# Sparse attention with a two-layer Mish network: a third set of PSUM banks for the last two blocks, and the last second product in half products

## The chip, the cores and the metric

One NeuronCore of one Trainium2 chip runs the whole program. The metric is the device time of one execution in microseconds (us): 319.56 us before the change, the median of 3 runs (319.44 to 320.93).

## The reference

Cut to what matters (8 batches, 8 heads, 576 positions, head size 64; 512 model columns, 2048 hidden ones):

```python
scores = np.matmul(q, k.transpose(0, 1, 3, 2)) / np.sqrt(64)
scores = np.where(masks, scores, -1e9)      # heads 0-3: the last 32 positions; heads 4-7: every 32nd
attn = softmax(scores)                      # over the last axis
x = (attn @ v).transpose(0, 2, 1, 3).reshape(4608, 512)
h = x @ w_in                                # 512 -> 2048: the first product
g = h * np.tanh(softplus(h))                # Mish
out = g @ w_out                             # 2048 -> 512: the second product
```

## The kernel before

The 4608 rows are cut into 9 blocks of 512 (t = 0 to 8). Attention works on one batch at a time and writes its result, transposed and in bf16, to `xT`; by the time that block 7 begins all 8 batches are done, so blocks 7 and 8 have only the network left.

**Seven products for eight.** Both matrix products use a scheme with seven products of half matrices where the plain way has eight (with sums of halves ahead and behind). The first product of a block is done in four groups g = 0 to 3 of 512 hidden columns. Each of its seven products is 4 matmuls of 128x128 by 128x256, so a group has 28 and a block 112. The second product has seven products n = 1 to 7 of 16 matmuls each (two halves u = 0, 1 of 8), again 112 in a block. Sums for the left and right sides are made on VectorE (DVE): `x_sum` from `xT` into `xs`, `g_sum` from `gT` into `gs`.

**Banks.** PSUM has 8 banks here: two sets of three, `SETS[0]` = (be0, al0, ee0) and `SETS[1]` = (be1, al1, ee1), and two banks of the attention, at0 and at1 (`A0`, `A1`). A group of the first product (`Mlp1.step`, L391) needs one bank each for be, al and ee: product 5 goes to ee and is copied to `s5`; product 1 goes to al and is copied to be by ScalarE (ACT, L401); product 6 is added to al and that copied to `s2`; 3 is added to ee, and DVE adds `s2` to it into `hh` (L119); 2 is added to be; 7 is added to al, and DVE adds `s5` to it into `hh`; 4 is added to al. Then ACT takes Mish of be ("U", L418), al ("W", L420) and `hh` ("H", L414) into `gT`. In the plan these steps are called a (products 5, 1), b (6, 3, 2), c (7), d (4). A word such as `b2` is step b of group 2. `SETS`, `s2`, `s5` and `hh` are chosen by z = (t + g + 1) % 2, so groups alternate between two sets.

The second product (`Mlp2.half`, L456) of the block ahead runs in the same stretch of the program, its 14 half products called `m` in the plan. It uses the three banks of one set: 1 starts al and ACT copies it to be (L477), 5 starts ee and is copied to `o5` (L479), 2 is added to be, 6 is added to al and copied to `o2` (L481), 3 is added to ee, 7 and 4 to al. DVE adds `o2` and `o5` into the output tile `osb`, ACT copies be and al (L490, L491), and SP stores 256 rows of 512 columns at a time (L501, 512 KB).

**Order.** It is written by hand. `run(plan, t)` (L662) issues the words of a plan one after the other, and every engine works through its own instructions in that order, waiting only where one needs another's result or space. `PLAIN` (L741) is the plan of t = 7 and t = 8:

```python
PLAIN = ("m m x0 m x1 m x2 g1 g2 m m m m g3 m m m m a0 m m b0 a1 x3 c0 U0 b1 d0 U1 W0 c1 a2 d1 W1 H0 "
         "a3 b2 c2 H1 b3 c3 d2 W2 H3 d3 n U2 U3 W3 H2")
```

After t = 8 the second product of block 8 stands alone (L749 to L756), in the order 1, 5, 6, 2, 7, 3, 4. Its last copy (L491) and the store behind it end the kernel.

Of the kernel before, what the change touches and what calls it, by code (L numbers as in the profile page):

```python
# [10 lines left out]
F32 = mybir.dt.float32  # L11
# [34 lines left out]
def kernel(ctx, tc, q, k, v, moe_w_in, moe_w_out, out):  # L46
    nc = tc.nc
    B, H, S, D = q.shape
# [4 lines left out]
    NBLK = NT // 512  # L53
    RT = RING * S
    PE, Po, Dv, Sc = nc.tensor, nc.gpsimd, nc.vector, nc.scalar
# [16 lines left out]
    s2, s5 = [[sb([128, 512], f"{n}{i}", F32) for i in range(2)] for n in ("s2", "s5")]  # L72
    o2, o5 = sb([128, 512], "o2", F32), sb([128, 512], "o5", F32)
    hh = [sb([128, 2, 512], f"hh{i}", F32) for i in range(2)]
# [33 lines left out]
    SETS = [[bank(f"{n}{i}") for n in ("be", "al", "ee")] for i in range(2)]  # L108
    A0, A1 = bank("at0"), bank("at1")
    PAIRS = ((A0, A1), SETS[0][1:3], SETS[1][1:3])  # L110

    def cast(eng, out_, in_):
        if eng is Sc:
# [4 lines left out]
    def add(eng, out_, a, b, op=ALU.add):  # L118
        eng.tensor_tensor(out=out_, in0=a, in1=b, op=op)  # L119
# [250 lines left out]
    class Mlp1:  # L370
# [19 lines left out]

        def step(self, s, g):  # L391
            z = (self.t + g + 1) % 2
            h = hh[z]
            be, al, E = [x[:] for x in SETS[z]]
            o = gT[:, 4 * g:4 * g + 4, :]
            two = lambda x: x.rearrange("p (u n) -> p u n", u=2)
            if s == "a":
                self.prod(5, g, E, True)
                cast(self.eng, s5[z][:], E)
                self.prod(1, g, al, True)  # L400
                Sc.copy(be, al)  # L401
            elif s == "b":
                self.prod(6, g, al, False)
                cast(self.eng, s2[z][:], al)
                self.prod(3, g, E, False)
                add(Dv, h[:, 0, :], E, s2[z][:])
                self.prod(2, g, be, False)
            elif s == "c":
                self.prod(7, g, al, False)
                add(Dv, h[:, 1, :], al, s5[z][:])  # L410
            elif s == "d":
                self.prod(4, g, al, False)
            elif s == "H":
                Sc.activation(  # L414
                    o[:, :, 256:512], h[:].rearrange("p i (u n) -> p (i u) n", u=2), AF.Mish
                )
            elif s == "U":
                Sc.activation(o[:, 0:2, 0:256], two(be), AF.Mish)  # L418
            elif s == "W":
                Sc.activation(o[:, 2:4, 0:256], two(al), AF.Mish)  # L420
# [15 lines left out]
    class Mlp2:  # L436
# [19 lines left out]
        def half(self, n, u):  # L456
            z = (self.t + 1) % 2
            be, al, E = [x[:] for x in SETS[z]]
            W = lambda kk, j: w_out[:, 8 * kk:8 * kk + 8, 256 * j:256 * j + 256]
            G = self.G  # L460
            L, R, bank, start = {
                1: (G(0, 0), W(0, 0), al, True), 2: (G(0, 1), W(1, 0), be, False),
                3: (G(1, 1), wos[:, 2], E, False), 4: (gs[:, 1], W(1, 1), al, False),
                5: (gs[:, 0], W(0, 1), E, True), 6: (gs[:, 1], wos[:, 0], al, False),
                7: (gs[:, 2], wos[:, 1], al, False),
            }[n]
            for c in range(8):
                mm(
                    bank[:, 256 * u:256 * u + 256], L[:, c, 128 * u:128 * u + 128], R[:, c, :],
                    start=(start and u == 0 and c == 0), stop=(c == 7),  # L470
                )
            if u == 0:
                return
            r = 512 * self.t
            halves = lambda x: x.rearrange("p (u d) -> p u d", u=2)
            if n == 1:
                Sc.copy(be, al)  # L477
            elif n == 5:
                Sc.copy(o5[:], E)  # L479
            elif n == 6:  # L480
                Sc.copy(o2[:], al)  # L481
            elif n == 3:
                osb = self.out_tile(1)
                add(Dv, osb[:, :, 0:256], halves(E), halves(o2[:]))
            elif n == 7:
                osb = self.out_tile(1)
                add(Dv, osb[:, :, 256:512], halves(al), halves(o5[:]))
            elif n == 4:
                osb = self.out_tile(0)
                Sc.copy(osb[:, :, 0:256], halves(be))  # L490
                Sc.copy(osb[:, :, 256:512], halves(al))  # L491
                self.store(0)
# [8 lines left out]
            nc.sync.dma_start(out[r:r + 256, :].rearrange("(u p) d -> p u d", u=2), self.osb[i][:])  # L501

        def steps(self, order=(1, 5, 2, 6, 3, 7, 4)):
            last = max(order, key=lambda n: order.index(n) if n in (3, 7) else -1)

            def go(n, u):
                self.half(n, u)
                if (n, u) == (last, 1):
                    self.store(1)
            return [lambda n=n, u=u: go(n, u) for n in order for u in range(2)]  # L510

    with tc.manual_schedule():
# [7 lines left out]
        def unread(n, to, w=512):  # L520
            for _ in range(n):
                mm(to[:, 0:w], wis[:, 0, 0, 0, 0:128], wis[:, 0:2, 0, 0, 0:w // 2], True)
# [139 lines left out]
        def run(plan, t):  # L662
            b = t + 1
            m1, m2, nxt = Mlp1(t), Mlp2(t - 1), Mlp2(t)
            at = Attn(b) if b < B else None
            ms = m2.steps() if t > 1 else []
            bank = [0]

            def v_steps():
                def pv(kind, r):  # L670
                    at.pv(kind, *r, (A0, A1)[bank[0] % 2])
                    bank[0] += 1

                def xt(kind, hf):
                    at.xt(kind, hf, (A0, A1)[bank[0] % 2], Dv)
                    bank[0] += 1
                P = lambda kd, r: (lambda: pv(kd, r))
                X = lambda kd, hf: (lambda: xt(kd, hf))
                return (
                    [P("s", r) for r in PV_S] + [X("s", 0), X("s", 1)]  # L680
                    + [P("l", r) for r in PV_L[:2]] + [X("l", 0)]
                    + [P("l", r) for r in PV_L[2:]] + [X("l", 1)]
                )
            vs_ = v_steps() if at else []
            JOBS = [("s", 0), ("s", 1), ("s", 2), ("l", 0), ("l", 1), ("l", 2)]
            for w in plan.split():
                c, n = w[0], int(w[1:]) if len(w) > 1 else 0
                if c in "abcdHUW":
                    m1.step(c, n)
                elif c == "p":  # L690
                    plain(t, n, six[n % 6], act=False)
                elif c == "y":
                    Sc.activation(gT[:, n, :], six[n % 6][:], AF.Mish)  # L693
                elif c == "k":
                    w_in_sums(2 * (n % 2), 2 * (n % 2) + 2, Dv, n // 2)
                elif c == "m":
                    ms.pop(0)()
                elif c == "x":
                    x_sum(t, n, Dv)
                elif c == "g":  # L700
                    m2.g_sum(n, Dv)
                elif c == "n":
                    nxt.g_sum(0, Dv, 0, 8)
                elif not at:
                    continue
                elif c == "e":
                    Sc.preload_act_table(AF.Exp)
                elif c == "f":
                    Sc.preload_act_table(AF.Mish)
                elif c == "q":  # L710
                    at.qk(*JOBS[n], PAIRS[n % 2 * (1 + (t + 1) % 2) if t > 1 else 0])
                    at.mask(*JOBS[n], Po)
                elif c == "v":
                    if vs_:
                        vs_.pop(0)()
                elif c == "s":
                    spread_v(Dv)
                    share_v(b, Dv)
                elif b + 1 >= B:
                    continue  # L720
                elif c == "D":
                    transpose_by_dma()
                elif c == "V":
                    load_vs(b + 1)
                    load_vl(b + 1)
                elif c == "R" and b + 2 < B:
                    load_qk(b + 2)
            assert not ms
            for w in vs_:
                w()  # L730
# [8 lines left out]
            "p11 y6 v p12 y7 v p13 y8 v p14 y9 v p15 y10 y11 y12 y13 y14 y15 n k1 k3 k5 k7"  # L739
        )  # L740
        PLAIN = (  # L741
            "m m x0 m x1 m x2 g1 g2 m m m m g3 m m m m a0 m m "
            "b0 a1 x3 c0 U0 b1 d0 U1 W0 c1 a2 d1 W1 H0 a3 b2 c2 H1 b3 c3 d2 W2 H3 d3 n U2 "
            "U3 W3 H2"
        )

        for t in range(1, NBLK):
            run(SECOND if t == 1 else MAIN if t + 1 < B else PLAIN, t)
        last = Mlp2(NBLK - 1)  # L749
        st = last.steps((1, 5, 6, 2, 7, 3, 4))  # L750
        last.g_sum(1, Dv)
        last.g_sum(2, Dv)
        for n, s in enumerate(st):
            s()
            if n == 5:
                last.g_sum(3, Dv)  # L756


# [28 lines left out]
```

## Time and profile before

| | |
|---|---|
| Median of 3 runs | 319.56 us |
| The profiled execution | 319.21 us |
| its span, first to last instruction | 317.4 us |
| mean granted TensorE clock | 0.983 |
| TensorE (PE) busy, whole span | 288.6 us (91%) |
| DVE, ACT busy, whole span | 205.7 us (65%), 201.2 us (63%) |
| Block 7's stretch (iteration t = 7) | about 245.8 to 272.5 us |
| Block 8's stretch (iteration t = 8) | about 272.5 to 299.2 us |
| Second product of block 8, alone | 299.2 to 312.6 us |
| Last copy, last store, end | 312.6 to 317.4 us |

How to read the profile: "L125 PE" are the matmuls (one helper line for all), "PEld" the weight loads, and `al<-xs,wis` names what is written and what is read, with the buffer numbers left out. `[0.28 <-ACT be L401]` after a row means that the engine sat idle for 0.28 us before it until ACT's instruction of line 401 on `be` was done. The profile models the end of a matmul: four matmuls of 256 columns show 0.60 us, while the next four start 0.44 us after them when nothing is waited for. So the true pause of PE between two rows is taken from their starts: the distance, less 0.109 us for each matmul of the first row.

### The profile page before, as it was taken

How to read it: one execution, taken by the hardware profiler on the slowest of the kernel's cores; microseconds unless marked ns; L12 is line 12 of the kernel's file. 1: busy time of each engine (PE TensorE's matmuls, PEld its weight loads, DVE VectorE, ACT ScalarE, POOL GpSimd, SP SyncE). 2: the span in 40 equal slices, each digit the busy share in tenths (PEclk: the TensorE clock that was granted, in tenths of full speed). 3: DMA queues.
4: the chain of work that ended last, by engine and by line, in shares of the span. 5: the costliest groups of instructions: out<-in, count | busy, mean ns of one | idle time of the engine just before them, and what ended most of it. 6: DMA issues, size and time to landing. Idle time of an engine off the chain costs nothing.

```text
span 317.4 us, 7701 instructions
## 1 busy us (share of the span) xinstructions
PE 288.6 (91%) x3218; PEld 228.4 (72%) x3224; DVE 205.7 (65%) x378; ACT 201.2 (63%) x357; POOL 116.9 (37%) x94
## 2 busy tenths in 40 slices
PE   8879679986994999999999999999999999999983
PEld 3554356833473798888888888988898887787773
DVE  2370396833888578768867794779578657747641
ACT  2587364357461768987887888788868526625630
POOL 8422355349504680298049607800930000000000
PEclk9999998999899899999999999999999999999999
DMA  7999999998990899589939993990030030002003
GB/s 105 182 206 206 204 183 138 95 243 130 150 115 0 114 231 169 32 142 214 169 41 176 205 137 64 213 107 0 2 134 2 0 119 15 3 34 101 0 2 133
DMA packets 97555, 35.85 MB, mean 113 GB/s; under 512 B 80800, under 2 KB 92896, under 8 KB 97520
## 3 DMA queue, kind: packets, MB, share of 16 engines
q0 software_dynamic: 60192, 17.67, 61.7%
q1 hardware_dynamic: 37184, 17.57, 27.7%
q8 instruction: 25, 0.41, 0.5%
q10 hardware_dynamic: 144, 0.12, 0.1%
q14 instruction: 10, 0.08, 0.1%
HBM read 35.51 MB, written 9.44 MB: 142 GB/s over the span
## 4 chain that ended last, share of the span: by engine, by line
PE 58%; DVE 16%; ACT 10%; DMA 10%; issue 4%; POOL 1%; DVEq 0%; ACTq 0%; POOLq 0%
PE al L125 29%; PE ee L125 14%; PE be L125 8%; DMA hh<-in_k_dram 7%; DVE hh L119 4%; DMA ql<-in_q_dram 3%; DVE gs L119 3%; ACT s L114 2%; ACT gT L414 2%; PE at L294 2%; PE at L125 2%; ACT gT L420 2%; DVE x_l L303 2%; DVE wis L119 1%; ACT be L401 1%
## 5 line engine op out<-in xcount | busy, mean ns | idle before, releaser
L125 PEld LDWEIGHTS <-w_in 128*128 128x128 bf16 x576 | 53.9, 98 | 23.6 <-issue 9.2
L271 POOL TENSOR_TENSOR Ps<-Ps,consts_sb 72x864 bf16<-72x864 bf16 (+1 forms) x20 | 36.8, 1859 | 87.1 <-ACT Ps L265 87.1
L125 PEld LDWEIGHTS <-gs 128*128 128x128 bf16 x576 | 55.8, 99 | 13.3 <-DVE gs L119 5.8
L125 PEld LDWEIGHTS <-gT 128*128 128x128 bf16 x432 | 41.0, 98 | 6.7 <-issue 0.4
L125 PE MATMUL al<-wos,gs 128*128 128x256 bf16 x288 | 36.4, 278 | 5.4 <-DVE gs L119 5.3
L125 PEld LDWEIGHTS <-wis 128*128 128x128 bf16 x348 | 33.1, 99 | 7.9 <-issue 3.3
L119 DVE TENSOR_TENSOR gs<-gT,gs 128x2048 bf16<-128x2048 bf16 x18 | 25.2, 1398 | 20.0 <-PE al L125 15.1
L271 POOL TENSOR_TENSOR Pl<-Pl,consts_sb 128x960 bf16<-128x960 bf16 (+1 forms) x20 | 33.5, 1701 | 0.8 <-ACT Pl L265 0.7
L125 PE MATMUL al<-xs,wis 128*128 128x256 bf16 x224 | 32.4, 272 | 0.8 <-ACT be L401 0.6
L125 PE MATMUL be<-xT,w_in 128*128 128x256 bf16 (+1 forms) x157 | 30.1, 311 | 2.8 <-ACT gT L693 1.3
L414 ACT ACTIVATE gT<-hh 128x1024 bf16<-128x1024 f32 x28 | 29.8, 1065 | 0.0
L125 PE MATMUL al<-xT,w_in 128*128 128x256 bf16 (+1 forms) x150 | 27.1, 299 | 1.9 <-ACT gT L420 1.7
L298 DVE RECIPROCAL rden<-at 72x7 f32<-72x7 f32 (+2 forms) x60 | 11.2, 187 | 21.6 <-PE at L294 18.1
L401 ACT COPY be<-al 128x512 f32<-128x512 f32 x28 | 16.4, 587 | 12.5 <-PE al L125 12.5
L420 ACT ACTIVATE gT<-al 128x512 bf16<-128x512 f32 x28 | 16.8, 599 | 11.0 <-PE al L125 11.0
L119 DVE TENSOR_TENSOR gs<-gT 128x2048 bf16<-128x2048 bf16 x18 | 21.9, 1217 | 0.0
L119 DVE TENSOR_TENSOR hh<-al,s 128x512 f32<-128x512 f32 x28 | 19.2, 684 | 2.9 <-PE al L125 2.5
L119 DVE TENSOR_TENSOR hh<-ee,s 128x512 f32<-128x512 f32 x28 | 19.2, 684 | 2.8 <-ACT s L114 1.9
L303 DVE TENSOR_TENSOR x_s<-at,rden 72x448 bf16<-72x448 f32 (+1 forms) x35 | 20.1, 574 | 1.2
L125 PE MATMUL ee<-wos,gT 128*128 128x256 bf16 x144 | 18.7, 277 | 0.0
L418 ACT ACTIVATE gT<-be 128x512 bf16<-128x512 f32 x28 | 15.9, 596 | 3.9 <-PE be L125 3.9
L125 PE MATMUL al<-xs,w_in 128*128 128x256 bf16 x112 | 16.8, 272 | 1.6 <-DVE hh L119 1.6
(137 smaller groups left out, 537.7 us busy)
## 6 DMA issues: line engine op xcount, KB each, us to landing
out_dram<-osb SPq DMA_DIRECT2D x18, 512.0 KB, 3.4
vraw<-in_v_dram POOLq DMA_DIRECT2D x8, 288.0 KB, 7.4
vl<-in_v_dram POOLq DMA_DIRECT2D x8, 288.0 KB, 9.6
w_in<-in_moe_w_in_dram POOLq DMA_DIRECT2D x4, 512.0 KB, 15.4
w_out<-in_moe_w_out_dram POOLq DMA_DIRECT2D x2, 1024.0 KB, 21.7
ql<-in_q_dram POOLq DMA_DIRECT2D x7, 288.0 KB, 12.9
kl<-in_k_dram POOLq DMA_DIRECT2D x5, 384.0 KB, 12.6
ks<-in_k_dram POOLq DMA_DIRECT2D x6, 288.0 KB, 10.0
```

Source lines behind the costliest of these rows:

```text
L114: Sc.copy(out_, in_)
L119: eng.tensor_tensor(out=out_, in0=a, in1=b, op=op)
L125: PE.matmul(o, lhsT=lhsT, rhs=rhs, start=start, stop=stop, skip_group_check=True)
L271: meng.tensor_tensor(out=pm, in0=pm, in1=mk[0:n, :].unsqueeze(1).unsqueeze(1).to_broadcast([n, 2, nu, w]), op=ALU.mult,)
L294: PE.matmul(po[:, n - n0, :], lhsT=pt[0:r, c0:c0 + 128], rhs=rhs, start=True, stop=True)
L298: Dv.reciprocal(rden[0:m, 0:nu], po[0:m, :, D])
L303: Dv.tensor_tensor(out=x[0:m, n0:n1, :], in0=po[0:m, :, 0:D], in1=rden[0:m, 0:nu].unsqueeze(2).to_broadcast([m, nu, D]), op=ALU.mult,)
L401: Sc.copy(be, al)
L414: Sc.activation(o[:, :, 256:512], h[:].rearrange("p i (u n) -> p (i u) n", u=2), AF.Mish)
L418: Sc.activation(o[:, 0:2, 0:256], two(be), AF.Mish)
L420: Sc.activation(o[:, 2:4, 0:256], two(al), AF.Mish)
```

## The change

It touches what is issued from t = 7 on.

- A third set of buffers is made as views of `ks` and `qs`, which hold rows of the attention: `hh[2]`, `s2[2]`, `s5[2]`. For t = 7 and 8 (`self.eng is Dv`), group 1 takes at1 as be, at0 as al, the ee bank of the set of group 0, and these buffers. Groups 0, 1, 2, 3 then have the buffers (t+1)%2, 2, t%2, (t+1)%2.
- At t = 7 one matmul of 512 columns is added that writes at1 (`unread(1, A1)`).
- `PLAIN` gets another order: the steps of the first product's groups 0 and 1 stand between the `m` of the second product, `x3` and `g1` stand earlier, and the last steps are ordered anew.
- The last second product (block 8) runs in half products: 1, 1, 5, 5, 2 (first half), 6, 6, 2 (second half), 7, 7, 3 (first half), 4, 4, 3 (second half). The second halves of 5 and 3 go to at0. Its output is stored in five pieces as they come: two of 128 rows by 256 columns from SP (product 3), three of 256 rows by 256 columns issued by ACT (products 2, 7, 4). Products 5 and 3 are copied or added 256 columns at a time.

```diff
+    wide = lambda x: flat(x[:].bitcast(F32))
+    hh.append(wide(ks).rearrange("p (i n) -> p i n", i=2))
+    s2.append(wide(qs)[:, 0:512])
+    s5.append(wide(qs)[:, 512:1024])
...
             z = (self.t + g + 1) % 2
+            be, al, E = [x[:] for x in SETS[z]]
+            if self.eng is Dv:
+                z = ((self.t + 1) % 2, 2, self.t % 2, (self.t + 1) % 2)[g]
+                be, al, E = [x[:] for x in ((A1, A0, SETS[(self.t + 1) % 2][2]) if g == 1 else SETS[z])]
             h = hh[z]
-            be, al, E = [x[:] for x in SETS[z]]
...
+            end = self.t == NBLK - 1
+            fresh = u == 0
+            if end and u and bank is E:
+                bank, fresh = A0[:], True
...
+            if end and n in (3, 5):
+                w = slice(256 * u, 256 * u + 256)
+                if n == 5:
+                    Sc.copy(o5[:, w], bank[:, w])
+                else:
+                    osb, r = self.out_tile(1), 512 * self.t + 256 + 128 * u
+                    add(Dv, osb[:, u, 0:256], bank[:, w], o2[:, w])
+                    nc.sync.dma_start(out[r:r + 128, 0:256], osb[:, u, 0:256])
+                return
             if u == 0:
                 return
-            r = 512 * self.t
+            if end and n in (2, 4, 7):
+                osb, k, r = self.out_tile(n == 7), slice(256 * (n > 2), 256 * (n > 2) + 256), 512 * self.t
+                src = (be if n == 2 else al).rearrange("p (u d) -> p u d", u=2)
+                if n == 7:
+                    r += 256
+                    add(Dv, osb[:, :, k], src, o5[:].rearrange("p (u d) -> p u d", u=2))
+                else:
+                    Sc.copy(osb[:, :, k], src)
+                Sc.dma_start(out[r:r + 256, k].rearrange("(u p) d -> p u d", u=2), osb[:, :, k])
+                return
...
+            if b == B:
+                unread(1, A1)
...
         PLAIN = (
-            "m m x0 m x1 m x2 g1 g2 m m m m g3 m m m m a0 m m "
-            "b0 a1 x3 c0 U0 b1 d0 U1 W0 c1 a2 d1 W1 H0 a3 b2 c2 H1 b3 c3 d2 W2 H3 d3 n U2 "
-            "U3 W3 H2"
+            "m m x0 g1 x1 m x2 x3 a0 m m m g2 m m b0 m g3 m m m c0 U0 a1 H0 m m b1 d0 W0 a2 c1 a3 b2 b3 d1 c3 "
+            "U2 H1 W1 U1 c2 d3 W3 U3 n d2 H2 W2 H3"
         )
...
-        st = last.steps((1, 5, 6, 2, 7, 3, 4))
+        st = last.steps("10 11 50 51 20 60 61 21 70 71 30 40 41 31")
...
-            if n == 5:
+            if n == 6:
                 last.g_sum(3, Dv)
```

More of the change, by code (lines that the diff above doesn't have):

```diff
@@ L469, in half @@
                     bank[:, 256 * u:256 * u + 256], L[:, c, 128 * u:128 * u + 128], R[:, c, :],
-                    start=(start and u == 0 and c == 0), stop=(c == 7),
+                    start=(start and fresh and c == 0), stop=(c == 7),
                 )
+            if end and n in (3, 5):
[7 more added lines that the diff above has]
+                return
             if u == 0:
                 return
-            r = 512 * self.t
+            if end and n in (2, 4, 7):
[8 more added lines that the diff above has]
+                return
             halves = lambda x: x.rearrange("p (u d) -> p u d", u=2)
@@ L503, in steps @@
         def steps(self, order=(1, 5, 2, 6, 3, 7, 4)):
+            if isinstance(order, str):
+                return [lambda n=int(w[0]), u=int(w[1]): self.half(n, u) for w in order.split()]
             last = max(order, key=lambda n: order.index(n) if n in (3, 7) else -1)
```

## The prediction

> **What bounds the kernel now.** I read the page's busy shares first, then the busy times by stretch for the part that the change touches, then the instructions in order of time in that part, then the end: the last store in the DMA view. Up to 245.8 us every engine's instructions are the same before and after, in the same order, so only 245.8 to the end (71.6 us of the span) can move.
>
> The stretches of blocks 7, 8 and the closing second product (length; then busy time of PE, PEld, DVE, ACT, POOL; PE's granted clock; DMA share; GB/s):
>
> ```profile
> 245.80:272.50 26.70, 25.56 (x227) 21.89 (x225) 18.34 (x27) 12.92 (x22) 0.00 (x0) 1.00 0.11 40
> 272.50:299.20 26.70, 25.52 (x226) 21.85 (x224) 17.92 (x27) 12.92 (x22) 0.00 (x0) 1.00 0.11 41
> 299.20:312.80 13.60, 12.58 (x114) 10.80 (x112) 5.63 (x6) 5.59 (x10) 0.00 (x0) 1.00 0.03 9
> ```
>
> PE is the bound: DVE works 18 of 26.7 us, ACT 13, DMA a tenth. The clock is full, so a matmul of 256 columns takes its 0.109 us (16 of them 1.75 us from start to start). A block has 224, which is 24.4 us; it takes 26.7. The 2.3 us between are pauses of PE, in which it waits for a copy, an add or a Mish. Those of block 8, in order of time (start, length, engine, line):
>
> ```profile
> 288.05 0.60 PE L125 MATMUL al<-xs,wis 128*128 128x256 bf16 x4
> 288.30 0.57 ACT L401 COPY be<-al 128x512 f32<-128x512 f32 x1 [1.65 <-PE al L125]
> ...
> 288.92 0.60 PE L125 MATMUL al<-xs,wis 128*128 128x256 bf16 x4 [0.28 <-ACT be L401]
> ...
> 293.45 0.60 PE L125 MATMUL al<-xT,w_in 128*128 128x256 bf16 x4 [0.35 <-ACT gT L420]
> ...
> 297.36 0.60 PE L125 MATMUL al<-xs,wis 128*128 128x256 bf16 x4
> ...
> 297.79 0.60 PE L125 MATMUL al<-xs,w_in 128*128 128x256 bf16 x4
> 298.05 0.68 DVE L119 TENSOR_TENSOR hh<-al,s 128x512 f32<-128x512 f32 x1
> ...
> 298.78 0.60 PE L125 MATMUL al<-xs,w_in 128*128 128x256 bf16 x4 [0.39 <-DVE hh L119]
> ...
> 303.69 1.92 PE L125 MATMUL al<-wos,gs 128*128 128x256 bf16 x16 [0.82 <-DVE gs L119]
> ...
> 312.64 0.59 ACT L491 COPY osb<-al 128x512 f32<-128x512 f32 x1 [4.61 <-PE al L125]
> ```
>
> The reader is to see the shape of a pause: a group of 4 is done, a reader starts 0.24 us after its last slot, works 0.6 to 0.7 us, PE may write again 0.05 us later, and between stands one other group (0.44 us). From start to start the pauses of block 8 are 0.21 (ahead of product 2 of the second product, at 276.19), 0.07, 0.44 (288.92), 0.09, 0.52 (293.45), 0.14, 0.28 (297.36), 0.55 (298.78): 2.30. Block 7 has the same eight, 2.26. The closing product has one, 0.99 (303.69), where product 6 waits for `gs`. Together **5.55 us**.
>
> **The change, part by part.** I laid the new order of each engine beside its waits and went through it with the durations of these rows: matmul 0.109; PE to reader 0.24; ACT on 512 columns 0.59, the next one 0.48 after its start; Mish of `hh` 1.06; DVE on 512 columns 0.69, the next one 0.60 after its start, 0.80 if it needs the first; `gs` 1.22; back to PE 0.05. The same way through the old order gives 5.4 of the 5.55 us of pauses, each in its place, so the method is good to some 0.15 us here.
>
> *What goes.* Groups 0 and 1 of a block no longer share banks with the second product of the block ahead (that has set t%2, they have the other set and at0, at1), so their steps stand between its halves, and each pause's cover grows from one group to at least a half product. Product 2 (0.21): eight matmuls of step a stand ahead, 0.87 more. Step b after the copy of line 401 (0.44): a0 and b0, and a1 and b1, now have at least 16 matmuls (1.75 us) between them where 0.88 is needed. Step a3 after "W" (0.52): d0's last matmul and a3's product 1 have 16 between. The small ones (0.09, 0.14, 0.28, 0.07) go the same way. Closing product (0.99): 8 matmuls of product 2 stand ahead of product 6, and the Mish order at the block's end is another; `gs` is ready 0.25 us ahead of its use.
>
> *What is late next.* At each block's end three pauses stay. The last writes are c3, c2, d3, d2: d3 waits for DVE's add on c3's bank, 0.24 + 0.69 + 0.05 = 0.98 after c3, with 0.44 of c2 as cover: 0.54, the pause of 298.78 again. d2 waits for the next add, which ends 0.60 after the first; d3 covers 0.44: 0.16. The second product's product 1 takes d3's bank, which ACT reads first: 0.24 + 0.59 + 0.05 = 0.88, with 0.16 + 0.44 as cover: 0.28. Together 0.98 a block, 1.96 for two. In the closing product 4 waits for the add of 7 (0.98, covered by 8 matmuls, 0.87): 0.10. The nearest waits without a pause have 0.16 (product 2 on the copy to be), 0.24 and 0.25 us to spare. Beyond `unread` the count of matmuls is the same; that one has 512 columns, 0.22 (four such rows start 0.86 apart early in the span). PE's term: 5.55 - 1.96 - 0.10 - 0.22 = **3.3 us**; from the old walk instead of the trace 3.15. I take 3.2. With hand-offs shorter or longer by 0.05 us it is 2.8 to 3.6: longer hand-offs hurt the old order more.
>
> *At nothing.* The sums moved ahead (`x3`, `g1`) lie on DVE, 8 us idle a block. The two copies of 256 columns for product 5 and the ACT stores lie where ACT idles: 4.61 us ahead of its last copy. A store holds its issuer 0.37 us (SP's rows). The ACT store of product 7 waits for DVE's add with the copy for product 4 queued behind it; that copy needs matmuls which end 1.7 us after the add. Without this cover it would cost up to 0.4.
>
> *The end.* T is the last matmul's slot end (310.69 + 16 x 0.109 = 312.43). Before, ACT copies from T + 0.2, the store is issued at T + 0.8 (313.25) and lands 3.1 later; the span ends 1.1 after that. The DMA views of the stretch 313 to 313.5 (packets, MB, share of 16 engines; then KB and us to landing), and SP's rows of the last two stores:
>
> ```profile
> q1 hardware_dynamic: 94, 0.19, 100.4%
> ...
> out_dram<-osb SPq DMA_DIRECT2D x1, 512.0 KB, 3.1
> ```
>
> ```profile
> 311.61 2.01 SPq L501 DMA_DIRECT2D out_dram<-osb  x2
> ```
>
> One store keeps all 16 engines busy: 94 packets of 2 KB in 0.5 us, 85 ns each on 16 engines. The store's 256 packets are 16 an engine, 1.36 us of its 3.1; the first moves 1.5 after the issue. After, the last piece is an add of 256 columns: 384 columns take 0.55 (L303), 512 take 0.69, so 0.41; it is issued at T + 0.7, 128 packets of 1 KB. The piece of product 4 (256 packets) was issued from ACT at T + 0.1. No row has 1-KB packets on this queue: half of 85 (43 ns) is the floor, the whole 85 the ceiling. The page's part 3 has the queue's rest: of 37184 packets, 17.57 MB and 27.7% of 16 engines' span, 4608 are these of 2 KB; the others have 250 bytes and 31 ns on the mean. On the line between, 1 KB takes 54, which I take. Both pieces are 24 packets an engine: from T + 1.6, 1.3 us, and 0.25 for the rest: landed at T + 3.1 where it was T + 3.9. **0.8 us** gained, 0 at 85 ns, 1.1 at 43.
>
> The Trainium skill, "DMA: Bandwidth & Descriptors", section "Issuing engines are not separate DMA queues", says that transfers issued from different engines interleave on the same 16 DMA engines and that only issue time is saved. It speaks against the two issuers: by it the pieces add up, as above; were ACT's queue apart, the last piece (8 packets an engine) would land at T + 2.9 and the gain be 1.0. The row with 100.4% for one store points the same way, but no run here shows two queues at once.
>
> **Sum.** 3.2 + 0.8 = 4.0 us. The profiled execution took 319.21 (span 317.4 and 1.8 around it), which gives **315.2**. The median of the runs is 0.35 above that execution, inside their spread of 1.5.
>
> **Rivals.** (1) *The end gives nothing*: 1-KB packets cost as 2-KB ones, or the pieces queue. For it: no row of their size. Against it: the line between the queue's short and long packets. 315.2 + 0.8 = 316.0. (2) *The pauses come back in other places*: groups 0 and 1 share one ee bank, group 1's al and be are the only spare pair, and DVE takes all copies to `s2`, `s5` in strict order behind the 1.22-us sums. If half of the 3.5 us that went come back, 317.0; if all, no change, about 319. For it: four waits have 0.25 us or less to spare. Against it: each is crossed with rows of the same instruction. (3) *Slower: DVE falls behind.* Place: DVE's queue in the first half of the block, where the sums `gs` and `xs` now stand ahead of the copies that free ee and al. PE has some 28 hand-overs in two blocks with 0.4 us to spare on the mean; if each comes 0.6 late, PE loses 28 x 0.2 = 5.6 us, as much as the 4.0 gained plus 1.6, the 0.5% that a measurement of this kernel can tell from no change. Under 0.55 late it isn't slower. That needs DVE's 0.69 to become nearly twice as long; the trace has it at 0.68 to 0.69 whatever else runs. If it decides: about 321. (4) *The change doesn't do what it says*, since an engine's order keeps the old wait: the orders as built show the moves, so this is a part of rival 2.
>
> **How the numbers follow.** Forecast 0.70, rival 1 0.11, half of the pauses back 0.09, no change 0.05, slower 0.05. Faster by over 0.5% is forecast, rival 1 and half: 0.90; the same 0.05; slower 0.05. Range: PE at 3.6 and the end at 1.1 give 319.21 - 4.7 = 314.5, and 0.3 less for the spread of runs, 314.2; upwards it takes rivals 1 and half of 2: 317.0.
>
> **What would show it.** In the trace after: no pause of PE over 0.1 us within a block until its last four groups, then 0.54, 0.16, 0.28; the last matmul 3.2 us earlier (312.4 to 309.2); product 6 of the closing product without a wait on `gs`; the last store landing 3.1 after the last matmul's slot instead of 3.9. Wrong it is if PE shows pauses in the first half of block 7 or 8 (rival 2 or 3), or if packets of 1 KB take 85 ns (rival 1).

## The result, and the profile after

315.25 us, the median of 4 runs (314.98 to 316.73), beside 320.15 before (4 runs, 319.44 to 320.93). The ratio is 0.9856, 95% interval 0.9814 to 0.9898. In a second set (`after_again`, below) it was 314.77 (5 runs) beside 320.43 (17 runs), 0.9838, interval 0.981 to 0.9867. The kernel is about 5 us, some 1.5%, faster.

The profiled execution took 314.98 us, its span 313.2. Busy times of the changed kernel by stretch, cut at the first matmul of block 6's second product (246.69, in before 245.80) and at the last matmul's slot end T (309.78, in before 312.44) (length; then busy time and instructions of PE, PEld, DVE, ACT, POOL; PE's granted clock; DMA share; GB/s):

```profile
0.00:16.00 16.00, 12.57 (x146) 6.18 (x147) 4.34 (x20) 6.22 (x11) 10.45 (x17) 0.89 1.15 144
16.00:40.00 24.00, 21.49 (x193) 11.69 (x194) 9.11 (x24) 15.36 (x31) 7.22 (x9) 0.86 1.26 204
...
246.69:309.78 63.09, 62.22 (x561) 54.66 (x559) 41.20 (x58) 32.13 (x53) 0.00 (x0) 1.00 0.12 45
309.78:313.20 3.42, 0.17 (x2) 0.00 (x0) 0.43 (x1) 0.00 (x0) 0.00 (x0) 0.98 0.34 115
```

The same stretches of before, which the prediction did not show:

```profile
0.00:16.00 16.00, 13.59 (x138) 6.72 (x140) 4.24 (x20) 6.23 (x11) 10.74 (x17) 1.00 1.12 144
16.00:40.00 24.00, 19.18 (x200) 10.67 (x202) 9.28 (x24) 15.58 (x32) 7.61 (x9) 1.00 1.25 205
...
245.80:312.44 66.64, 63.50 (x562) 54.53 (x559) 41.89 (x58) 31.26 (x51) 0.00 (x0) 1.00 0.09 33
312.44:317.40 4.96, 0.16 (x2) 0.00 (x0) 0.00 (x0) 0.59 (x1) 0.00 (x0) 0.94 0.56 213
```

Three things are to be read off. From the first of those matmuls to T it is 63.1 us where it was 66.6: 3.5 less, against which stands the 0.2 of the added matmul, issued ahead of the stretch. From T to the end it is 3.4 where it was 5.0: 1.6 less. Together 4.9. And the part that the change does not touch is no constant: blocks 7 and 8 began 0.9 us later in this execution than in the one of before, and the change accounts for the added matmul's 0.2 alone. (So T is 309.8, and not the 309.2 that the prediction names.) Over eleven profiled executions that start lay between 245.8 and 248.6 us, and the one of before was the earliest. PE's clock early in the span differs too (0.86 against 1.00 from 16 to 40 us), but that it is the whole cause is not shown; the last section comes back to it. So I compare kernels by these two stretches, and by medians. The stretches hold still: 63.09 and 63.08 up to T in two executions of the changed kernel, and 3.38 to 3.41 behind T in five with its closing product.

The changed kernel's instructions in order of time, at the end of block 7 and at the kernel's end (here and below, a view's last row counts only the instructions inside its window):

```profile
269.40 1.04 PE L129 MATMUL al<-xs,wis 128*128 128x256 bf16 x8
...
270.78 1.20 PE L129 MATMUL al<-xs,w_in 128*128 128x256 bf16 x8 [0.34 <-DVE hh L123]
...
271.38 0.31 PEld L129 LDWEIGHTS <-w_in 128*128 128x128 bf16 x3 [0.17 <-issue]
...
272.07 1.14 PE L129 MATMUL al<-w_out,gT 128*128 128x256 bf16 x9
```

```profile
301.80 1.91 PE L129 MATMUL al<-wos,gs 128*128 128x256 bf16 x16
...
307.17 1.91 PE L129 MATMUL al<-w_out,gs 128*128 128x256 bf16 x16
...
309.98 0.43 DVE L123 TENSOR_TENSOR osb<-at,o 128x256 f32<-128x256 f32 x1 [2.32 <-PE at L129]
```

From start to start (the eight matmuls of 269.40 take 0.87, those of 270.78 too), PE pauses 0.51 before 270.78, 0.16 in the midst of that row, where its weight loads stop at 271.38, and 0.25 before 272.07. These are step d of group 3, step d of group 2 and the next second product, as in the prediction. Block 8 has the same three. Product 6 of the closing product (301.80) waits for nothing; product 4 (307.17) waits 0.13. All the pauses from 246.7 on are 1.97 us, where there were 5.54.

### The profile page after: what moved, and what is told of

It is laid out like the page before. It is cut to its first block, busy times and chain, and to the rows that moved or that the text cites. A ratio compares the mean times of both kernels' runs of the same rounds, so it can differ in the third digit from the quotient of the medians.

```text
span 313.2 us, 7708 instructions
## 1 busy us (share of the span) xinstructions
PE 289.6 (92%) x3225; PEld 229.1 (73%) x3225; DVE 205.9 (66%) x379; ACT 201.6 (64%) x358; POOL 116.6 (37%) x94
## 4 chain that ended last, share of the span: by engine, by line
PE 62%; DVE 15%; DMA 10%; ACT 8%; issue 3%; POOL 1%; DVEq 0%; POOLq 0%; ACTq 0%
PE al L129 30%; PE ee L129 15%; PE be L129 9%; DMA hh<-in_k_dram 7%; PE at L129 4%; DVE hh L123 4%; DMA ql<-in_q_dram 3%; ACT s L118 2%; DVE gs L123 2%; PE at L298 2%; DVE x_l L307 2%; ACT gT L427 1%; DVE wis L123 1%; ACT gT L421 1%; DVE x_s L307 1%
## 5 line engine op out<-in xcount | busy, mean ns | idle before, releaser
L129 PE MATMUL al<-xs,wis 128*128 128x256 bf16 x208 | 30.1, 272 | 0.0
L421 ACT ACTIVATE gT<-hh 128x1024 bf16<-128x1024 f32 x26 | 27.7, 1064 | 0.0
L427 ACT ACTIVATE gT<-al 128x512 bf16<-128x512 f32 x26 | 15.5, 598 | 9.2 <-PE al L129 9.2
L123 DVE TENSOR_TENSOR hh<-al,s 128x512 f32<-128x512 f32 x26 | 17.6, 684 | 2.7 <-PE al L129 2.1
L123 DVE TENSOR_TENSOR hh<-ee,s 128x512 f32<-128x512 f32 x26 | 17.8, 684 | 2.5 <-ACT s L118 1.8
L129 PE MATMUL be<-w_out,gT 128*128 128x256 bf16 x144 | 18.4, 281 | 0.0
L425 ACT ACTIVATE gT<-be 128x512 bf16<-128x512 f32 x26 | 14.9, 594 | 4.9 <-PE be L129 4.9
L129 PE MATMUL ee<-wos,gT 128*128 128x256 bf16 x136 | 17.4, 273 | 0.0
L129 PE MATMUL al<-w_out,gs 128*128 128x256 bf16 x144 | 17.4, 272 | 0.0
```

Of the source, the lines that this page charges most:

```text
L129: PE.matmul(o, lhsT=lhsT, rhs=rhs, start=start, stop=stop, skip_group_check=True)
L421: Sc.activation(o[:, :, 256:512], h[:].rearrange("p i (u n) -> p (i u) n", u=2), AF.Mish)
```

## The experiments

In each, T, the stretch up to it and the end behind it are meant as above.

**The two halves of the change, each alone.** `e1_plan` has the third set and the new plan with the closing product of before; `e2_tail` has the closing product alone.

```diff
 e1_plan, from the changed kernel
-            end = self.t == NBLK - 1
+            end = False
-        st = last.steps("10 11 50 51 20 60 61 21 70 71 30 40 41 31")
+        st = last.steps((1, 5, 6, 2, 7, 3, 4))
-            if n == 6:
+            if n == 5:
 e2_tail, from the changed kernel: PLAIN as before, and
-            if self.eng is Dv:
+            if False:
-            if b == B:
+            if False:
                 unread(1, A1)
```

> The third set and the new order of the plan alone; the closing second product and its stores as before. Theory (every pause is a hand-off chain less the work that covers it; the two halves of the change add up): the pauses of blocks 7 and 8 fall from 2.3 to 0.93 us each, the one of the closing product falls from 0.99 to about 0.63, because the Mish order at the end of block 8 is another; with 0.22 for the added matmul the last matmul comes 2.65 us earlier, and from its slot's end to the end of the span it is 5.0 us as before. 319.6 to 320.2 before gives 317.0 to 317.5. Rival (the end is where it is gained, the pauses come back elsewhere): under 1 us faster.

> The closing second product in half products with its pieces stored as they come, alone; blocks 7 and 8 with two sets and the old plan, without the added matmul. Theory: the pauses of blocks 7 and 8 stay at 2.3 us each; in the closing product 0.99 becomes 0.22 (product 2 on the copy to be) and 0.10 (product 4), so the last matmul comes 0.7 us earlier; from its slot's end to the span's end it is 3.4 us in place of 5.0. Together 2.3 us faster, 317.3 to 317.9. Rival (the shorter end needs the matmuls ahead of it undisturbed): 0.7 us.

Measured: `e1_plan` 317.03 (ratio 0.9905, 0.9877 to 0.9933), `e2_tail` 318.29 (0.9929, 0.99 to 0.9959), beside 320.64 before. In the traces `e1_plan` has 63.61 up to T and 5.00 behind it, `e2_tail` 65.96 and 3.39. Against 66.63 and 5.00 that is 3.0 (2.8 with the added matmul) and 2.3 us less. Both theories hold in both of these numbers: the pauses do not come back, and the shorter end does not need the new plan. The median of `e2_tail` lies 0.4 above the 317.9 that was expected at most. The one pause that the plan leaves to the old closing product, in `e1_plan`:

```profile
298.58 1.91 PE L129 MATMUL ee<-w_out,gs 128*128 128x256 bf16 x16
300.96 1.26 PE L129 MATMUL al<-wos,gs 128*128 128x256 bf16 x10 [0.47 <-DVE gs L123]
```

16 matmuls from 298.58 end at 300.32, so 0.64 is paused, 0.63 was expected. The eight matmuls of product 2 that the new closing order puts ahead cover it.

**The banks without the order.** `e3_banks` keeps the third set, and takes the old plan and the old closing product.

```diff
 from e1_plan
-            "m m x0 g1 x1 m x2 x3 a0 m m m g2 m m b0 m g3 m m m c0 U0 a1 H0 m m b1 d0 W0 a2 c1 a3 ...
+            "m m x0 m x1 m x2 g1 g2 m m m m g3 m m m m a0 m m b0 a1 x3 c0 U0 b1 d0 U1 W0 c1 a2 ...
```

> The third set of banks and buffers alone: old plan, old closing product. Theory (banks are worth nothing without the order, and hurt where group 3 takes the set of the next second product): group 3 now sits in the set that the second product behind it starts with, and the old order takes Mish of that bank last, so its product 1 waits some 2.3 us; product 5 of group 2 waits 0.9 for the ee bank that group 1 shares with group 0. Slower by 4.2 us, about 324. Rival (the spare banks themselves remove the pauses): 1 to 3 us faster than before.

Measured: 327.23, ratio 1.0214 (1.019 to 1.0239), 6.6 us slower than before. The sign and the two places named are those of the theory, the size is not: 4.2 were expected. The trace has 73.52 up to T, 6.9 more. PE at the end of block 7, and the busy times of the stretches around it:

```profile
272.68 0.60 PE L129 MATMUL al<-xs,w_in 128*128 128x256 bf16 x4 [0.36 <-DVE hh L123]
275.41 3.43 PE L129 MATMUL al<-w_out,gT 128*128 128x256 bf16 x16 [2.13 <-ACT gT L427]
278.68 0.49 PE L129 MATMUL ee<-w_out,gs 128*128 128x256 bf16 x3
```

```profile
272.00:275.40 3.40, 0.92 (x7) 0.52 (x6) 2.85 (x6) 3.04 (x6) 0.00 (x0) 0.96 0.00 0
275.40:278.80 3.40, 3.39 (x18) 2.44 (x18) 2.36 (x2) 0.91 (x1) 0.00 (x0) 0.53 0.02 5
278.80:282.00 3.20, 3.20 (x32) 2.87 (x30) 0.00 (x0) 1.16 (x2) 0.00 (x0) 1.00 0.00 0
```

The pause of 2.3 us stands where it was expected (2.30 from start to start). But the 16 matmuls behind it take 3.27 us, not 1.75: the seventh column of the second row of stretches shows a granted clock of 0.53. After the pause PE runs at half clock for 3.4 us, which costs 1.5 a block, 3.0 in all; 9.3 us of pauses and these 3.0 on 560 matmuls of 0.109 make the 73.5. The pauses alone are 3.8 more than before, 4.0 with the added matmul, close to the 4.2 expected; what the theory lacked is the half clock. So spare banks alone, given out in this way, are a loss, and the rival falls: the gain comes with the order. The new order with the old two sets was not run; that it needs the banks is read from the waits and not shown.

**The end.** `e4_whole_stores` stores the closing output in the two stores of 512 KB of before, `e9_last_whole` only its second half (products 7 and 3), and `e5_sp_only` issues all five pieces from SP.

```diff
 e9_last_whole, from the changed kernel (e4_whole_stores also replaces the stores of products 2 and 4 by self.store(0))
-                    nc.sync.dma_start(out[r:r + 128, 0:256], osb[:, u, 0:256])
+                    if u:
+                        self.store(1)
...
+                if n != 7:
                     Sc.dma_start(out[r:r + 256, k].rearrange("(u p) d -> p u d", u=2), osb[:, :, k])
 e5_sp_only, from the changed kernel
-                Sc.dma_start(out[r:r + 256, k].rearrange("(u p) d -> p u d", u=2), osb[:, :, k])
+                nc.sync.dma_start(out[r:r + 256, k].rearrange("(u p) d -> p u d", u=2), osb[:, :, k])
```

> The changed kernel with the closing product's output stored as before the change: two stores of 512 KB from SP, after product 4 and after the last half of 3; the arithmetic's order as changed. Theory (the end is packets on 16 shared engines: 0.9 us from issue to the first packet, 47 ns a KB and engine, 0.4 behind the last): both stores' 3.3 us of packets stand behind T - 0.1 + 0.9, so the span ends 5.5 us after the last matmul's slot in place of 3.4: 2.1 us slower than the changed kernel, 317.3. Rival (it is the earlier issue and a fixed landing time that count, not the size): 0.2 us slower.

> The changed kernel, but the 256 rows of products 7 and 3 stored as before, in one store of 512 KB from SP after the last half of 3; the pieces of products 2 and 4 from ACT as changed. It sizes the last store alone. Theory (0.9 us from issue to the first packet, which the prediction put at 1.5; 2-KB packets of 85 ns and more, 1.65 for 256 of them; 0.45 behind; 0.9 to 1.1 to the end): issued at T + 0.8, first packets at T + 1.7, when those of product 4's piece are done; the span ends 4.8 us after the last matmul's slot in place of 3.4: 1.4 us slower than the changed kernel. The prediction's own terms (1.5 to the first packet) would give T + 5.2. Rival (product 4's piece holds the engines, whole or not): the end stays within 0.4 us of the changed kernel's.

> The changed kernel with all five closing pieces issued from SP, none from ACT. Theory (the pieces share 16 engines whoever issues them, and SP is free when each is ready): no difference, within 0.2 us of the changed kernel. Rival (two issuing queues run side by side): the last piece stands behind the one of product 4, 0.4 to 0.8 us slower.

| | median (us) | ratio to before, interval | up to T | behind T |
|---|---|---|---|---|
| changed kernel | 315.25 | 0.9856, 0.9814 to 0.9898 | 63.09 | 3.40 |
| `e4_whole_stores` | 318.91 | 0.9953, 0.9927 to 0.9979 | 63.09 | 5.76 |
| `e9_last_whole` | 316.94 | 0.9855, 0.9777 to 0.9933 | 63.09 | 4.87 |
| `e5_sp_only` | 315.79 | 0.9868, 0.9841 to 0.9894 | 63.08 | 3.37 |

With arithmetic and order unchanged, the end follows what stands in the queues: 5.76 (5.5 expected) with two whole stores, 4.87 (4.8) with one, 3.40 with pieces. Storing the last 256 rows piece by piece is worth 1.5 us; the rivals (0.2 and 0.4) fall. These sizes are read from the traces. The runs of `e4_whole_stores` lie far apart (316.96 to 320.67), and its median, 1.6 above the expected 317.3, isn't explained by its end alone: its profiled execution began block 7 at 248.6, 1.9 later than the changed kernel's. The DMA row (busy tenths in 40 slices) shows how an end is made. First before, from 311.6 to 316.4, a slice being 0.12 us; then the changed kernel, from 309.6 to 312.8, a slice being 0.08:

```profile
DMA  0000000398999989998108899999989960000000
```

```profile
DMA  0000000000001699999999999984000000000000
```

In before SP issues at 311.61 and 313.25; packets move from the eighth and from the twenty-second slice, 0.9 us after each issue. In the changed kernel ACT issues product 4's piece at 309.72 and SP the last at 310.44; the engines are full from 310.7 to 311.7 without a gap. So the 0.9 of the last piece (310.44 to 311.3) lies under the packets of the piece ahead of it. `e5_sp_only` gives the same end, 0.03 less: it makes no difference which engine issues. That is what the Trainium skill says in "DMA: Bandwidth & Descriptors", section "Issuing engines are not separate DMA queues", and here it agrees. The pair is a weak test of it, since the packets of the last two pieces overlap by less than 0.2 us. The pieces ahead say more: SP issues the first one of product 3 at 307.69, and its first packet moves at 308.79, 1.1 us later and not 0.9, while packets of ACT's piece of product 7 move from 308.05 to 308.9. By time alone neither `e5_sp_only` nor `e9_last_whole` can be told from the changed kernel (their intervals overlap with its own; of what `e5_sp_only`'s profiled execution took, 0.6 us more than `after_again` lie ahead of block 7, where the programs are the same).

**The chain less its cover.** `e6_d1_late` moves four matmuls at the end of a block (and takes two Mish steps, U1 and U3, in other places); `e7_copies_twice` makes DVE do 16 copies twice. `after_again` is the changed kernel itself beside them.

```diff
 e6_d1_late, from the changed kernel
-            "... b1 d0 W0 a2 c1 a3 b2 b3 d1 c3 U2 H1 W1 U1 c2 d3 W3 U3 n d2 H2 W2 H3"
+            "... b1 d0 W0 U1 a2 c1 a3 b2 b3 c3 U2 H1 c2 d1 W1 d3 W3 n U3 d2 H2 W2 H3"
 e7_copies_twice, from the changed kernel (and the same for s2)
-                cast(self.eng, s5[z][:], E)
+                for _ in range(2 if self.eng is Dv else 1):
+                    cast(self.eng, s5[z][:], E)
```

> The changed kernel again, as a base for the next three on the same chip. Theory: 315.2, ratio to before 0.985; last matmul 63.1 us after the first one of iteration 7's second product, 3.4 us from its slot's end to the span's end, whatever the clock does in the first 40 us.

> The changed kernel with another order at the end of a block: step d of group 1 stands ahead of step d of group 3 and no longer ahead of step c of group 3, Mish of group 1's be is taken earlier. Theory (a pause is chain less cover, and 4 matmuls moved into a place give it 0.44 more cover): 0.20 new ahead of c3, 0.54 at d3 falls to 0.10, 0.16 and 0.28 stay; 0.24 less a block, last matmul 0.5 us earlier, 314.7. Rival (DVE's or ACT's queue is what ends last there): the pauses' sum stays at 0.93 a block.

> The changed kernel with each of DVE's copies to s5 and s2 done twice in blocks 7 and 8 (16 copies of 0.6 us more). It prices the prediction's slower rival, DVE falling behind. Theory: the covers of the first half of a block take the first copies' lateness, then 0.7 appears ahead of product 3 of group 2 and 2.3 ahead of product 7 of group 3 in each block: 6.0 us slower than the changed kernel, about 321, slower than before the change. Rival (DVE has 8 us idle a block, so 4.8 us more lies in it): under 1.5 us slower than the changed kernel.

`after_again`: 314.77, 63.09 up to T and 3.39 behind, as expected. `e6_d1_late`: 314.24 (6 runs, 313.83 to 316.96), ratio 0.9835 (0.9798 to 0.9871), 62.67 up to T. PE at the end of its block 7:

```profile
268.47 0.60 PE L129 MATMUL be<-xT,w_in 128*128 128x256 bf16 x4
269.13 1.03 PE L129 MATMUL al<-xs,wis 128*128 128x256 bf16 x8
270.00 0.60 PE L129 MATMUL at<-xs,w_in 128*128 128x256 bf16 x4
270.52 1.20 PE L129 MATMUL al<-xs,w_in 128*128 128x256 bf16 x8
271.80 1.47 PE L129 MATMUL al<-w_out,gT 128*128 128x256 bf16 x12
```

The pauses are 0.22 (before 269.13), 0.08 (before 270.52), 0.16 and 0.25: 0.71 a block in place of 0.92, where 0.74 was expected. Four matmuls (0.44) moved under a pause of 0.51 took 0.43 of it and opened 0.22 where they had stood. It is the fastest kernel of the study by its trace, 0.4 us under the changed one; the difference of the medians, 0.5, is less than the spread of the runs.

`e7_copies_twice`: 321.09, ratio 1.0014 (0.999 to 1.0039): as slow as before the change. It has 69.23 up to T, 6.1 more than the changed kernel, 6.0 expected. The end of its block 7 and of its block 8:

```profile
269.13 0.60 PE L129 MATMUL ee<-xT,wis 128*128 128x256 bf16 x4 [0.36 <-DVE s L120]
...
272.57 1.22 PE L129 MATMUL al<-xs,wis 128*128 128x256 bf16 x5 [1.97 <-DVE s L120]
```

```profile
297.99 0.60 PE L129 MATMUL ee<-xT,wis 128*128 128x256 bf16 x4 [0.37 <-DVE s L120]
...
301.42 1.03 PE L129 MATMUL al<-xs,wis 128*128 128x256 bf16 x8 [1.97 <-DVE s L120]
```

The pauses sit where they were expected, 0.52 (0.7 expected) and 2.13 (2.3). In block 7 the longer one is again followed by half clock (five matmuls take 1.22 in the row of 272.57), in block 8 it isn't (eight take 1.03). So the 6.0 was met in part by luck: the longer pauses make 5.3 (twice what block 8 has more than the changed kernel), and the half clock of block 7, which the expectation does not have, adds 0.8. The copies are 4.8 us more a block on an engine with 8 us idle there, and cost 3 us a block, so idle time on the mean is no cover, and the rival falls. The price of the prediction's slower rival was near, 6.1 for its 5.6, but it comes as two pauses a block and not as 0.2 at each of 28 hand-overs.

## Why the prediction was right, and where it was not

It said 315.2 and 315.25 was measured, but not with the gain that it had worked out: 4.0 us were predicted, 4.9 came. Two errors of nearly the same size met, and that the time came out to 0.05 us is luck.

- *The pauses (3.3 worked out, 3.2 taken)*: right. 5.54 became 1.97, and 0.21 went to the added matmul: 3.36. Each pause that was to stay stayed: 0.54, 0.16, 0.28 were predicted, 0.51, 0.16, 0.25 measured; 0.10 in the closing product was 0.13. `e1_plan` and `e6_d1_late` show that these numbers follow the order and not the place.
- *The end (0.8)*: the mechanism was right, the size was not; 1.6 was measured. The term that failed is "the first moves 1.5 after the issue". It is 0.9: in the DMA row of before the packets of the store issued at 313.25 begin in the twenty-second slice, 314.1, right behind those of the store ahead of it, and were taken for that store's. With 0.9, product 4's piece is nearly done when the last piece's packets come, and the last piece lands at T + 2.5, not T + 3.1. The packets of 1 KB took 47 ns (54 was taken), and the waits behind the last landing 0.9 in place of 1.1. `e9_last_whole` was reckoned with 0.9 and came within 0.1.
- *The base (319.21)*: the sum was made against one execution, which was a quick one. The median of before is 320.15, 320.43, 320.6 and 320.64 in four sets. The prediction saw 0.35 between that execution and the median of three runs and left it out. It was 0.9 to 1.4 us, and took back what the end had been given too little.
- *The cost at nothing*: right. No pause stands at the moved sums, the half copies or ACT's stores.
- *The rivals*: 1 falls by the 47 ns and by `e9_last_whole`, 2 by the trace after. 3 was not the case; its price is near, its even spread over 28 hand-overs is not what DVE's lateness does (`e7_copies_twice`).

## What to carry to other kernels

Where an engine is busy 95% of a stretch, list its pauses from start to start and write each as a chain (hand-off, reader, hand-back) less the work that stands under it: this foretold the place of every pause over 0.1 us, and the length to 0.03 us, in four kernels (the changed one, `e1_plan`, `e2_tail`, `e6_d1_late`). In `e7_copies_twice` it had the two new pauses to 0.18, in `e3_banks` the two that it named to 0.04, and in both it lacked the half clock. More buffers without an order that uses them can cost more than they bring. At the end of a kernel count what the last transfer waits behind, and make the last pieces small; and make the sum against the median of many runs, not against one profiled execution.

## What the runs showed of the hardware

PE's clock went to half after a single pause of 2.1 to 2.3 us, and stayed there for 3.4 us, in full-speed work on both sides. In `e3_banks` both pauses of 2.30 did this; in `e7_copies_twice` one pause of 2.13 did and the other, of the same length, did not. The Trainium skill, "TensorE: Matmul & The Clock Gate", section "What's actually happening", speaks of an idle window of some 3.4 us that runs freely. A free-running window fits the two unequal cases; but a pause well under 3.4 us was enough here, where PE had also been idle for part of the 3.4 us before. The traces bear the window out: the half clock of `e3_banks` begins at 275.15 and at 305.87, 30.72 us apart, nine times 3.41. In the 3.41 us ahead of these two PE was busy 1.18 and 1.08 us, ahead of the one of `e7_copies_twice` (272.60) 1.44. Counted on from there in steps of 3.41, the window that holds most of block 8's pause (299.91 to 303.32) has 1.54, and no half clock followed. Which share has to be busy was not tried.

The same instructions ahead of block 7 took up to 2.6 us more in one execution than in another (245.8 in before, 248.6 in `e4_whole_stores`, 0.2 of it the added matmul). Half clock goes along with it in part: from 16 to 40 us 1.00 was granted in `before`, 0.86 in `after`, 0.93 in `e4_whole_stores`, and there from 40 to 120 us 0.87 where the other two have 0.94. But the clock column early in the span is not to be trusted alone. `e7_copies_twice` has 1.00 from 0 to 40 us, as `before` has, and began block 7 at 247.2; its four matmuls of 23.07 take 1.77 us from start to start, where four of the same form took 0.86 in `before`:

```profile
23.07 1.98 PE L129 MATMUL be<-xT,w_in 128*128 128x512 bf16 x4
24.84 1.06 PE L129 MATMUL al<-xT,w_in 128*128 128x512 bf16 x2
```

```profile
25.57 1.02 PE L125 MATMUL be<-xT,w_in 128*128 128x512 bf16 x4 [0.73 <-ACT xT L114]
26.43 0.59 PE L125 MATMUL al<-xT,w_in 128*128 128x512 bf16 x2
```

What decides how long the early part takes was not tried.
